# Mask distances built on GpSimd ahead of its first load, and the last store issued from ScalarE's queue for a whole block

## The chip, the core and the metric

One core of a Trainium2 chip. The metric is the device time of one execution in microseconds (us). A single number is the median of several executions. The span that a profile shows is about 2 us shorter than the device time of the same execution (315.6 against 317.4 for the kernel before).

## The reference

Sliding-window attention with ALiBi slopes, then a feed-forward layer with a squared ReLU. Cut to what matters:

```python
# q, k, v: (8 batches, 8 heads, 576 positions, 64), float32
scores = q @ k.T / 8 + slopes * -(i - j)          # only where 0 <= i - j < 128
attn   = softmax(scores) @ v                      # -> x: (4608, 512)
r      = maximum(x @ w_in, 0)                     # w_in: (512, 2048)
out    = (r * r) @ w_out                          # w_out: (2048, 512) -> (4608, 512)
```

576 positions are four blocks of 128 and one of 64 for each batch. The half blocks of two batches share one range of 128 columns of the transposed x.

## The kernel before

The kernel is written as a list of tasks with the engines that may run each, a priority key and dependencies; a small planner orders them ahead of time, and the instructions are emitted in that order. Three places matter here. First, the head: the distances `dist` (key position minus query position) come from an iota on GpSimd. VectorE turns them into the identity for transposes and into the distances with the forbidden side pushed to 1e6; ScalarE exponentiates them into the masks.

```python
def build_iota():
    nc.gpsimd.iota(dist, pattern=[[-128, 2], [1, 128]], base=128, channel_multiplier=-1, ...)
def build_ident():
    nc.vector.tensor_single_scalar(ident, dist[:, 1], 0.0, op=ALU.is_equal)
def build_dist(part):                              # part 1 in the head, part 0 about 18 us later
    op, lim = ((ALU.is_ge, float(window)), (ALU.is_lt, 0.0))[part]
    nc.vector.tensor_scalar(far[:, part], dist[:, part], lim, 1.0e6, op0=op, op1=ALU.mult)
    nc.vector.tensor_tensor(dist[:, part], dist[:, part], far[:, part], op=ALU.add)
```

Second, the loads. Block 0's k and q come through the queues of SyncE and ScalarE into `stage`. Everything else is loaded through GpSimd, which converts float32 to bfloat16 on the way: v of block 0, k, q and v of blocks 1 and 2 ("the seven small loads", 128 KB each as stored), then the weights in quarters of 512 KB (`w_in_sb` is the first of them).

```python
FIRST = ["b0", "b1", "b2", "i0", "i1", "o0", "i2", "o1", "b3", ...]    # b: block, i/o: quarter of w_in/w_out
def fetch_v():
    nc.gpsimd.dma_start(tile_of(s_v[m])[0:n, :, 0:D], source(v, m))
l_v = plan.add({"POOL": 890.0}, key + 0.2, fetch_v, [t_zero] if kb == HALF else [], [s_v[m]], ...)
```

Third, the tail. The last output range is cut into 384 and 128 columns, each evacuated from PSUM and stored by SyncE, with one store for each block in the range. The last range of the kernel before holds the half blocks of the last two batches, so each cut needs two stores of 64 rows.

```python
    jobs.append(("half", [len(seq), len(seq) + 1]))
    ranges.append([(b, HALF), (b + 1, HALF)])
    seq += ranges[-1]
# ... (cut) ...
def store():
    for i, (b, kb) in enumerate(ranges[4 * g + t]):
        n = blk[kb]
        nc.sync.dma_start(out[b * S + kb * 128:b * S + kb * 128 + n, lo:hi], so.tile[i * 64:i * 64 + n, 0:hi - lo])
```

The softmax here doesn't subtract the row's maximum and nothing guards it: scores larger than these inputs give would overflow.

Of the kernel before, what the change touches and what calls it, by code (L numbers as in the profile page):

```python
# [26 lines left out]
CUT = 384  # L27
SIZE = {"kq": 4, "v": 9, "kqT": 7, "P": 3, "x": 3}
DUE = {**{m: 200.0 * m - 1e5 for m in range(40)}, **{7: -40.0}}


def FUSED(g, u):
# [24 lines left out]
class Plan:  # L57
# [24 lines left out]
        return t  # L82

    def order(self):
        used = {tag: [] for tag in self.bufs}
        free, cand, left = {}, {}, {}
        for t in self.tasks:
            left[t] = len(t.deps)
            for d in t.deps:
                d.users.append(t)  # L90
            for e in t.engs:
                free.setdefault(e, self.BEGIN[e])
                cand.setdefault(e, [])
        for t in self.tasks:
            if not left[t]:
                for e in t.engs:
                    cand[e].append(t)

        def avail(t):
            at = t.ready  # L100
            if t.dma is not None:
                lane = self.lanes["SW" if "POOL" in t.engs else "HW"]
                if len(lane) >= self.LANES:
                    at = max(at, lane[-self.LANES])
            taken = {}
            for s in t.acq:
                u, n = used[s.tag], self.bufs[s.tag]
                j = len(u) + taken.get(s.tag, 0) - n
                taken[s.tag] = taken.get(s.tag, 0) + 1
                if j >= len(u):  # L110
                    raise RuntimeError("a task takes more than its ring")
                if j >= 0:
                    if u[j].left:
                        return None
                    at = max(at, u[j].freed)
            return at

        done = []
        n_all = len(self.tasks)
        while len(done) < n_all:  # L120
            best = None
            for e, c in cand.items():
                could = []
                for t in c:
                    a = avail(t)
                    if a is not None:
                        could.append((max(a, free[e]), t.key, t.seq, t))
                lo = None
                if could:
                    by = min(could)[0] + self.NEAR.get(e, 0.0)  # L130
                    got = min((x for x in could if x[0] <= by), key=lambda x: x[1:3])
                    lo = (got[:3], got[3])
                if lo is not None and (best is None or lo[0][:2] < best[0][:2]):
                    best = (lo[0], e, lo[1])
            if best is None:
                raise RuntimeError("plan is stuck: " + repr([
                    (e, t.name, t.key, [s.tag for s in t.acq]) for e, c in cand.items() for t in c][:40]))
            (st, _, _), e, t = best
            t.eng, t.start = e, st
            dur = t.engs[e]  # L140
            if e == "PE" and st < self.FILL_UNTIL:
                t.gap = max(0.0, st - max([free[e]] + [used[s.tag][len(used[s.tag]) - self.bufs[s.tag]].freed
                                                       for s in t.acq if len(used[s.tag]) >= self.bufs[s.tag]]))
            if t.dma is not None:
                at = max(st + self.FIRST[e], self.dma_free)
                self.dma_free = at + t.dma
                t.end = self.dma_free + (self.LAND[e] if t.lat is None else t.lat)
                for _ in range(t.count):
                    self.lanes["SW" if e == "POOL" else "HW"].append(t.end)
            else:  # L150
                t.end = st + dur + (self.LAT[e] if t.lat is None else t.lat)
            free[e] = st + dur
            for x in t.engs:
                cand[x].remove(t)
            for s in t.acq:
                s.idx = len(used[s.tag]) % self.bufs[s.tag]
                used[s.tag].append(s)
            for s in t.rel:
                s.left -= 1
                s.freed = max(s.freed, t.end)  # L160
            for u in t.users:
                left[u] -= 1
                at = st + dur if u.engs.keys() == {e} and t.dma is None else t.end
                if "SP" in u.engs and t.dma is None:
                    at += self.TO_SP
                u.ready = max(u.ready, at)
                if not left[u]:
                    for x in u.engs:
                        cand[x].append(u)
            done.append(t)  # L170
        done.sort(key=lambda t: (t.start, t.seq))
        return done
# [3 lines left out]
def kernel(  # L176
    ctx: ExitStack, tc: tile.TileContext, q, k, v, moe_w_in, moe_w_out, out
):
    nc = tc.nc
# [20 lines left out]
    for b in range(0, B, 2):  # L200
        for x in [(b + i, kb) for i in range(2) for kb in range(1, HALF)]:
            jobs.append(("full", [len(seq)]))
            seq.append(x)
            ranges.append([x])
        jobs.append(("half", [len(seq), len(seq) + 1]))
        ranges.append([(b, HALF), (b + 1, HALF)])
        seq += ranges[-1]
    at = {x: m for m, x in enumerate(seq)}
    NBLK = len(seq)
    col = {}  # L210
# [86 lines left out]

    def build_dist(part):
        op, lim = ((ALU.is_ge, float(window)), (ALU.is_lt, 0.0))[part]
        nc.vector.tensor_scalar(far[:, part], dist[:, part], lim, 1.0e6, op0=op, op1=ALU.mult)  # L300
        nc.vector.tensor_tensor(dist[:, part], dist[:, part], far[:, part], op=ALU.add)

    t_dist, t_mask, last_mask = [None, None], [[], []], None
    for part in (1, 0):
        key = EARLY + 2 if part else -1e5 + 1100
        t_dist[part] = plan.add({"DVE": 430.0}, key, lambda part=part: build_dist(part), [t_ident], name="dist",
                                later=0.0 if part else 18000.0)
        for p in range(H):
            def build_mask(p=p, part=part):
                nc.scalar.activation(masks[:, p, part], dist[:, part], AF.Exp, bias=0.0,  # L310
                                     scale=-(2.0 ** (-8.0 * (head_at[p] + 1) / H)))
            t_mask[part].append(plan.add({"ACT": act(128)}, key + 1 + p, build_mask, [t_dist[part]], name="mask"))

    def ones(ts):
        for t in ts:
            nc.vector.memset(t[:, :, D:D + 1], 1.0)
    t_ones = [plan.add({"DVE": 320.0}, EARLY + 3, lambda: ones(tiles["v0"][0:2]), name="ones"),
              plan.add({"DVE": 900.0}, -1e5 + 300, lambda: ones(tiles["v0"][2:]), name="ones", later=11000.0),
              plan.add({"DVE": 1200.0}, -1e5 + 900, lambda: ones(tiles["v"]), name="ones", later=20000.0)]


    halves = [m for m in range(NBLK) if seq[m][1] == HALF]
# [34 lines left out]
    def load_block(m, key):  # L357
# [32 lines left out]

        def fetch_v():
            nc.gpsimd.dma_start(tile_of(s_v[m])[0:n, :, 0:D], source(v, m))  # L392
        l_v = plan.add({"POOL": 890.0}, key + 0.2, fetch_v, [t_zero] if kb == HALF else [], [s_v[m]],
                       dma=ns, name=f"lv{m}")
        t_v[m] = [l_v, t_ones[0 if m < 2 else 1 if m < B else 2]]

# [25 lines left out]
    def transpose_kq(m, due):  # L422
# [12 lines left out]
        for i in range(2):  # L435
# [14 lines left out]
            for c0, c1 in pieces:  # L450
                def evac(i=i, st=st, c0=c0, c1=c1, e=len(evs[i])):
# [4 lines left out]
                    else:  # L456
# [1 line left out]
                    copy(evs[i][e], o, src)  # L458
                w = (c1 - c0) * n
                evs[i].append(plan.add({"ACT": act(w), "DVE": dve_p(w, 1 if split else 2)}, due - 58, evac,  # L460
                                       [t_tp[i]] + evs[i], [], [st], name=f"ev{m}.{i}"))
        last["tp"] = t_tp[1]
        t_kqT[m] = [[evs[0][0], evs[1][0]], evs[0] + evs[1]]

# [188 lines left out]
    def relu_square(g, slot, last_mm, key, out_of, fused):  # L653
# [12 lines left out]
        else:  # L666
            srt = Slot("rt")

            def relu():
                srt.tile = work.tile([128, 512], BF16, tag="rt", bufs=3, name="rt")  # L670
                nc.scalar.activation(srt.tile, slot.tile, AF.Relu, bias=0.0, scale=1.0)  # L671
            tr = plan.add({"ACT": act(512)}, key, relu, [last_mm], [srt], [slot], name=f"relu{g}")
            ts = plan.add({"DVE": dve(512, 2)}, key, lambda: square(srt.tile), [tr] + g_sq[g][:1], [], [srt],
                          name=f"sq{g}")
        g_sq[g].append(ts)
        return ts

# [54 lines left out]
    def o_piece(g, t, some, key, z, lo, hi, end):  # L732
# [4 lines left out]
        def emit():  # L737
# [3 lines left out]
            for fc in range(4 * some[0], 4 * some[-1] + 4):  # L741
# [2 lines left out]
        tm = plan.add({"PE": 4 * len(some) * mm(hi - lo)}, key, emit,  # L744
                      [prev] + [x for p in some for x in [t_wout[p]] + sq_of[g, t, p]],
                      [slot] if some[0] == 0 else [], [g_slots[g]] if t == 3 and some[-1] == 3 and end else [],
                      name=f"o{g}.{t}.{some[-1]}")
        o_slots[g, t, z][1] = tm
        if some[-1] < 3:
            return  # L750
# [2 lines left out]
        def evac():  # L753
            so.tile = work.tile([128, d_model], FP32, tag="osb", bufs=3, name="osb")
            copy(te, so.tile[:, 0:hi - lo], slot.tile[:, 0:hi - lo])
        te = plan.add({"ACT": act(hi - lo), "DVE": dve_p(hi - lo)}, key, evac, [tm], [so], [slot], name=f"oe{g}.{t}")

        def store():
            for i, (b, kb) in enumerate(ranges[4 * g + t]):
                n = blk[kb]  # L760
                nc.sync.dma_start(out[b * S + kb * 128:b * S + kb * 128 + n, lo:hi],
                                  so.tile[i * 64:i * 64 + n, 0:hi - lo])
        plan.add({"SP": 530.0}, key, store, [te], [], [so], dma=680.0 * (hi - lo) / 512, lat=1000.0, name=f"st{g}.{t}")

    for i, item in enumerate(work_list):
        {"unit": unit, "fc": fc_step, "o": o_part}[item[0]](*item[1:], 4 * i)
# [36 lines left out]
```

## Time and profile before

| quantity | value |
|---|---|
| device time, median of 6 runs | 317.51 us (317.29 to 317.97) |
| span of the profiled run | 315.6 us |
| PE busy | 306.2 us, 97% |
| first load issued by GpSimd | 1.34 us |
| first weight matmul | 14.34 us |
| last matmul ends | 311.0 us |
| last store lands | 314.5 us |

The page of the kernel before shows the bound. In the first line, busy time and share; in the rows below, the busy share of each fortieth of the span in tenths.

```profile
PE 306.2 (97%) x2810; PEld 176.3 (56%) x2810; DVE 173.4 (55%) x494; ACT 173.5 (55%) x340; POOL 105.4 (33%) x131
...
PE   6989999999999999999999999999999999999994
...
DMA  9999999999999999999999949962211000011112
```

TensorE is at nine tenths or more from the fourth slice to the last but one. What can still be won or lost in a change like this lies in the first three slices and the last one. The first slices are also those in which the DMA engines are busy without a break, so TensorE's head hangs on loads.

The timeline of GpSimd in the kernel before (start, duration, engine, instruction). A load's duration here is the time for which GpSimd issues it, not the transfer:

```profile
0.84 0.34 POOL L287 IOTA dist<- 128x256 f32 x1 [0.39 <-POOLq L787]
1.34 1.03 POOL L392 DMA_DIRECT2D vf<-in_v_dram  x1 [0.16 <-issue]
2.36 0.89 POOL L387 DMA_DIRECT2D kq<-in_k_dram  x1
3.24 0.90 POOL L387 DMA_DIRECT2D kq<-in_q_dram  x1
4.11 0.90 POOL L392 DMA_DIRECT2D vf<-in_v_dram  x1
...
7.57 1.55 POOL L340 DMA_DIRECT2D w_in_sb<-in_moe_w_in_dram  x2
```

From its first load on GpSimd is never idle here: after the first, one load follows another every 0.87 us. The first weight load is the eighth, issued at 7.57 and landed at 14.23. (A load has landed when its data is complete; the "lag" below is the time from the start of its issue to its landing.)

The chain of waits that ended last, in its first 45 us (start, duration, what), goes over these loads:

```profile
0.84 0.34 POOL dist L287
1.18 0.16 issue
1.34 1.03 POOL vf L392
2.37 1.76 POOL kq L387 x2
4.13 0.87 POOL vf L392
5.01 1.75 POOL kq L387 x2
6.76 0.88 POOL vf L392
7.63 0.68 POOL w_in_sb L340
8.31 9.45 DMA w_in_sb<-in_moe_w_in_dram
17.75 0.28 issue
18.04 14.42 DMA w_out_sb<-in_moe_w_out_dram
```

The tail of the kernel before, all engines but TensorE's weight loads, cut to the last output:

```profile
309.48 1.54 PE L742 MATMUL o<-w_out_sb,g 128*128 128x384 bf16 x19
...
310.17 0.56 DVE L271 COPY osb<-o 128x384 f32<-128x384 f32 x1 [1.85 <-PE o L742]
310.75 2.41 SPq L761 DMA_DIRECT2D out_dram<-osb  x4
311.06 0.29 DVE L271 COPY osb<-o 128x128 f32<-128x128 f32 x1 [0.34 <-PE o L742]
```

SyncE issues four stores one after the other, from 310.75 to 313.16. The data of the last one was ready at 311.35, but it was issued only at 312.57. That is 1.55 us after the last matmul.

### The profile page before, as it was taken

The numbers are of one execution on the slowest core, as the hardware profiler recorded it, in microseconds if no ns is written. First come the engines' busy times: TensorE is split into PE (matmuls) and PEld (weight loads), VectorE is DVE, ScalarE is ACT, GpSimd is POOL, SyncE is SP. The second block draws the span as 40 slices with busy tenths as digits, with TensorE's granted clock in tenths as the row PEclk, the third lists the DMA queues.
The fourth block names the chain that finished last, engine by engine and source line by source line (L and its number), as shares of the span: only waits on it lengthen the run. The fifth ranks groups of instructions, "written<-read, shape, count | busy, mean of one in ns | idle before, by whom it ended". The sixth has DMA issues, their size and how long they took to land.

```text
span 315.6 us, 7140 instructions
## 1 busy us (share of the span) xinstructions
PE 306.2 (97%) x2810; PEld 176.3 (56%) x2810; DVE 173.4 (55%) x494; ACT 173.5 (55%) x340; POOL 105.4 (33%) x131
## 2 busy tenths in 40 slices
PE   6989999999999999999999999999999999999994
PEld 2878767667777655555555455545444444444442
DVE  3755567666767667676676666666663222222111
ACT  4676466668566635675655665557743444444300
POOL 8825498643623837206756007200000000000000
PEclk9799999999999999999999999999999999999999
DMA  9999999999999999999999949962211000011112
GB/s 129 190 204 190 169 194 178 141 174 127 208 178 127 172 136 194 160 118 143 160 199 160 145 96 137 190 114 70 50 52 50 35 34 33 35 33 44 57 69 66
DMA packets 164130, 39.14 MB, mean 124 GB/s; under 512 B 154752, under 2 KB 159616, under 8 KB 164096
## 3 DMA queue, kind: packets, MB, share of 16 engines
q0 software_dynamic: 114656, 18.10, 84.3%
q1 hardware_dynamic: 49152, 20.33, 34.3%
q8 instruction: 22, 0.36, 0.5%
q10 hardware_dynamic: 288, 0.26, 0.3%
q14 instruction: 12, 0.10, 0.1%
HBM read 36.70 MB, written 9.44 MB: 146 GB/s over the span
## 4 chain that ended last, share of the span: by engine, by line
PE 86%; DMA 9%; POOL 2%; issue 0%; DVE 0%; POOLq 0%
PE o L742 38%; PE h L716 27%; PE h L700 10%; PE pv L566 6%; PE s L499 5%; DMA w_out_sb<-in_moe_w_out_dram 5%; DMA w_in_sb<-in_moe_w_in_dram 3%; DMA kq<-in_q_dram 2%; POOL kq L387 1%; POOL vf L392 1%; PE tp L443 0%; PE xp L608 0%; POOL w_in_sb L340 0%; POOL dist L287 0%; DVE osb L271 0%
## 5 line engine op out<-in xcount | busy, mean ns | idle before, releaser
L742 PE MATMUL o<-w_out_sb,g 128*128 128x512 bf16 (+2 forms) x592 | 143.0, 373 | 0.3 <-DMA w_out_sb<-in_moe_w_out_dram 0.3
L671 ACT ACTIVATE rt<-h 128x512 bf16<-128x512 f32 x144 | 85.8, 609 | 94.2 <-PE h L716 69.9
L662 DVE TENSOR_TENSOR g<-rt 128x512 bf16<-128x512 bf16 x144 | 60.2, 421 | 75.7 <-ACT rt L671 75.6
L716 PE MATMUL h<-xT,w_in_sb 128*128 128x512 bf16 x384 | 96.7, 379 | 0.0
L742 PEld LDWEIGHTS <-g 128*128 128x128 bf16 x592 | 54.0, 98 | 55.9 <-issue 0.4
L523 ACT ACTIVATE P<-s 128x512 bf16<-128x512 f32 (+1 forms) x136 | 67.0, 582 | 9.0 <-PE s L499 8.9
L716 PEld LDWEIGHTS <-w_in_sb 128*128 128x128 bf16 x384 | 35.2, 98 | 39.3
L531 DVE TENSOR_TENSOR P<-P,masks 128x512 bf16<-128x512 bf16 (+1 forms) x112 | 44.6, 405 | 15.1 <-ACT P L523 10.3
L700 PE MATMUL h<-xT,w_in_sb 128*128 128x128 bf16 (+1 forms) x512 | 46.8, 246 | 1.1 <-ACT rt L671 0.7
L387 POOL DMA_DIRECT2D kq<-in_k_dram x39 | 33.5, 858 | 33.5 <-DMA kqT<-kq 28.2
L392 POOL DMA_DIRECT2D vt<-in_v_dram x32 | 27.0, 847 | 45.8 <-PE pv L566 43.5
L700 PEld LDWEIGHTS <-w_in_sb 128*128 128x128 bf16 x512 | 38.6, 98 | 5.2 <-DMA w_in_sb<-in_moe_w_in_dram 1.4
L387 POOL DMA_DIRECT2D kq<-in_q_dram x39 | 33.5, 859 | 9.1 <-PE h L700 4.8
L588 DVE TENSOR_TENSOR x<-pv,rec 128x256 bf16<-128x256 f32 (+1 forms) x80 | 33.5, 422 | 2.6
L566 PEld LDWEIGHTS <-P 128*128 128x128 bf16 (+1 forms) x576 | 26.0, 101 | 15.2 <-DVE x L588 1.7
L584 DVE RECIPROCAL rec<-pv 128x4 f32<-128x4 f32 (+1 forms) x80 | 14.2, 179 | 21.0 <-PE pv L566 18.1
L566 PE MATMUL pv<-vt,P 128*128 128x65 bf16 (+1 forms) x448 | 24.6, 194 | 0.0
L273 ACT ACTIVATE osb<-o 128x512 f32<-128x512 f32 x23 | 13.9, 606 | 8.0 <-PE o L742 7.7
L499 PEld LDWEIGHTS <-kqT 64*128 64x128 bf16 x448 | 12.4, 94 | 7.3 <-issue 7.2
L271 DVE COPY osb<-o 128x512 f32<-128x512 f32 (+2 forms) x14 | 9.2, 654 | 12.8 <-PE o L742 12.6
L499 PE MATMUL s<-kqT 64*128 64x128 bf16 (+1 forms) x256 | 15.6, 210 | 0.0
L499 PE MATMUL s<-kqT,kqT 64*128 64x128 bf16 (+1 forms) x192 | 11.4, 209 | 0.0
(42 smaller groups left out, 103.1 us busy)
## 6 DMA issues: line engine op xcount, KB each, us to landing
out_dram<-osb SPq DMA_DIRECT2D x32, 256.0 KB, 4.0
kq<-in_k_dram POOLq DMA_DIRECT2D x31, 128.0 KB, 7.2
kq<-in_q_dram POOLq DMA_DIRECT2D x31, 128.0 KB, 7.4
vt<-in_v_dram POOLq DMA_DIRECT2D x24, 128.0 KB, 7.4
w_in_sb<-in_moe_w_in_dram POOLq DMA_DIRECT2D x4, 512.0 KB, 11.0
w_out_sb<-in_moe_w_out_dram POOLq DMA_DIRECT2D x4, 512.0 KB, 14.4
vf<-in_v_dram POOLq DMA_DIRECT2D x8, 128.0 KB, 6.7
out_dram<-osb SPq DMA_DIRECT2D x6, 128.0 KB, 2.3
```

The lines of the kernel that those rows point to most:

```text
L387: nc.gpsimd.dma_start(view(kq[s_kq[m].idx], i), source(src, m, split))
L392: nc.gpsimd.dma_start(tile_of(s_v[m])[0:n, :, 0:D], source(v, m))
L499: nc.tensor.matmul(sS[2 * g2 + r].tile[:, jj * 256 + c0:jj * 256 + c0 + w], tile_of(s_kqT[mk])[rows, c, :], tile_of(s_kqT[mq])[rows, C + c ...
L523: nc.scalar.activation(flat(Pt[sP.idx]), sS[i].tile.rearrange("p (j t) -> p j t", j=2)[:, :, lo:hi], AF.Exp, bias=0.0, scale=scale)
L531: nc.vector.tensor_tensor(flat(Pt[sP.idx]), flat(Pt[sP.idx]), flat(masks), op=ALU.mult)
L566: nc.tensor.matmul(sv.tile[0:n, hi * (D + 1):(hi + 1) * (D + 1)], Pt[sP.idx][:, place(h)].rearrange("p t q -> p (t q)")[:, w], tile_of(s_v ...
L588: nc.vector.tensor_tensor(xt[sx.idx][0:n, hf * 256:(hf + 1) * 256].rearrange("p (h e) -> p h e", h=4), heads(sv)[0:n, :, 0:D], sr.tile[0:n ...
L662: nc.vector.tensor_tensor(o, i, i, op=ALU.mult)
L671: nc.scalar.activation(srt.tile, slot.tile, AF.Relu, bias=0.0, scale=1.0)
L700: nc.tensor.matmul(slot.tile[:, f * w:(f + 1) * w], w_in_sb[:, cc, fc * 128:(fc + 1) * 128], xT[:, cc, lo:lo + w], start=cc == 0, stop=cc ...
L716: nc.tensor.matmul(slot.tile, w_in_sb[:, cc, fc * 128:(fc + 1) * 128], xT[:, cc, g * 512:(g + 1) * 512], start=cc == 0, stop=cc == C - 1)
L742: nc.tensor.matmul(slot.tile[:, 0:hi - lo], gt[:, fc, t * 128:(t + 1) * 128], w_out_sb[:, fc, lo:hi], start=fc == 0, stop=fc == FCB - 1)
```

## The change

The intent: in the tail, let the last range be a whole block (one store for each cut instead of two) and let ScalarE, which is idle by then, evacuate the last 128 columns and store them from its own queue. In the head, take the two instructions for the distances off VectorE and put them on GpSimd between its iota and its first load. The core of the diff, cut and with long lines shortened; the rest renames tasks, removes an unused variable and adds an empty table of priority offsets:

```diff
         jobs.append(("half", [len(seq), len(seq) + 1]))
-        ranges.append([(b, HALF), (b + 1, HALF)])
-        seq += ranges[-1]
+        seq += [(b, HALF), (b + 1, HALF)]
+        ranges.insert(len(ranges) - (b + 2 == B), seq[-2:])
 ...
     def build_dist(part):
         op, lim = ((ALU.is_ge, float(window)), (ALU.is_lt, 0.0))[part]
-        nc.vector.tensor_scalar(far[:, part], dist[:, part], lim, 1.0e6, op0=op, op1=ALU.mult)
-        nc.vector.tensor_tensor(dist[:, part], dist[:, part], far[:, part], op=ALU.add)
+        e = nc.gpsimd if part else nc.vector
+        e.tensor_scalar(far[:, part], dist[:, part], lim, 1.0e6, op0=op, op1=ALU.mult)
+        e.tensor_tensor(dist[:, part], dist[:, part], far[:, part], op=ALU.add)
 ...
-        t_dist[part] = plan.add({"DVE": 430.0}, key, lambda part=part: build_dist(part), [t_ident], name="dist",
-                                later=0.0 if part else 18000.0)
+        t_dist[part] = plan.add({"POOL": 700.0} if part else {"DVE": 430.0}, key, lambda part=part: build_dist(part),
+                                [t_iota if part else t_ident], name=f"dist{part}", later=0.0 if part else 18000.0)
 ...
-        l_v = plan.add({"POOL": 890.0}, key + 0.2, fetch_v, [t_zero] if kb == HALF else [], [s_v[m]],
+        l_v = plan.add({"POOL": 890.0}, key + 0.2, fetch_v, [t_zero] if kb == HALF else [t_dist[1]], [s_v[m]],
 ...
-        te = plan.add({"ACT": act(hi - lo), "DVE": dve_p(hi - lo)}, key, evac, [tm], [so], [slot], ...)
+        engs = {"ACT": act(hi - lo), "DVE": dve_p(hi - lo)}
+        if end and (g, t) == (NG - 1, 3):
+            del engs["DVE"]
+        te = plan.add(engs, key, evac, [tm], [so], [slot], ...)
+        final = end and (g, t) == (NG - 1, 3)
 ...
-                nc.sync.dma_start(out[...], so.tile[...])
-        plan.add({"SP": 530.0}, key, store, ...)
+                (nc.scalar if final else nc.sync).dma_start(out[...], so.tile[...])
+        plan.add({"ACTQ" if final else "SP": 530.0}, key, store, ...)
```

A comparison of the built programs shows that the order of TensorE's instructions is the same in both kernels. The two distance instructions are the only ones that move in the head, and the last copy and the last stores the only ones in the tail.

More of the change, by code (lines that the diff above doesn't have):

```diff
@@ L29 @@
 DUE = {**{m: 200.0 * m - 1e5 for m in range(40)}, **{7: -40.0}}
+ADJ = {}
 def FUSED(g, u):
@@ L84, in order @@
     def order(self):
+        for t in self.tasks:
+            t.key += ADJ.get(t.name, 0.0)
         used = {tag: [] for tag in self.bufs}
@@ L299, in build_dist @@
         op, lim = ((ALU.is_ge, float(window)), (ALU.is_lt, 0.0))[part]
-        nc.vector.tensor_scalar(far[:, part], dist[:, part], lim, 1.0e6, op0=op, op1=ALU.mult)
-        nc.vector.tensor_tensor(dist[:, part], dist[:, part], far[:, part], op=ALU.add)
-    t_dist, t_mask, last_mask = [None, None], [[], []], None
+        e = nc.gpsimd if part else nc.vector
+        e.tensor_scalar(far[:, part], dist[:, part], lim, 1.0e6, op0=op, op1=ALU.mult)
+        e.tensor_tensor(dist[:, part], dist[:, part], far[:, part], op=ALU.add)
+    t_dist, t_mask = [None, None], [[], []]
     for part in (1, 0):
         key = EARLY + 2 if part else -1e5 + 1100
-        t_dist[part] = plan.add({"DVE": 430.0}, key, lambda part=part: build_dist(part), [t_ident], name="dist",
-                                later=0.0 if part else 18000.0)
+        t_dist[part] = plan.add({"POOL": 700.0} if part else {"DVE": 430.0}, key, lambda part=part: build_dist(part),
+                                [t_iota if part else t_ident], name=f"dist{part}", later=0.0 if part else 18000.0)
         for p in range(H):
@@ L311, in build_mask @@
                                      scale=-(2.0 ** (-8.0 * (head_at[p] + 1) / H)))
-            t_mask[part].append(plan.add({"ACT": act(128)}, key + 1 + p, build_mask, [t_dist[part]], name="mask"))
+            t_mask[part].append(plan.add({"ACT": act(128)}, key + 1 + p, build_mask, [t_dist[part]], name=f"mask{part}.{p}"))
     def ones(ts):
@@ L316, in ones @@
             nc.vector.memset(t[:, :, D:D + 1], 1.0)
-    t_ones = [plan.add({"DVE": 320.0}, EARLY + 3, lambda: ones(tiles["v0"][0:2]), name="ones"),
-              plan.add({"DVE": 900.0}, -1e5 + 300, lambda: ones(tiles["v0"][2:]), name="ones", later=11000.0),
-              plan.add({"DVE": 1200.0}, -1e5 + 900, lambda: ones(tiles["v"]), name="ones", later=20000.0)]
+    t_ones = [plan.add({"DVE": 320.0}, EARLY + 3, lambda: ones(tiles["v0"][0:2]), name="ones0"),
+              plan.add({"DVE": 900.0}, -1e5 + 300, lambda: ones(tiles["v0"][2:]), name="ones1", later=11000.0),
+              plan.add({"DVE": 1200.0}, -1e5 + 900, lambda: ones(tiles["v"]), name="ones2", later=20000.0)]
     halves = [m for m in range(NBLK) if seq[m][1] == HALF]
@@ L460, in transpose_kq @@
                 evs[i].append(plan.add({"ACT": act(w), "DVE": dve_p(w, 1 if split else 2)}, due - 58, evac,
-                                       [t_tp[i]] + evs[i], [], [st], name=f"ev{m}.{i}"))
+                                       [t_tp[i]] + evs[i], [], [st], name=f"ev{m}.{i}.{c0}"))
         last["tp"] = t_tp[1]
@@ L671, in relu @@
                 nc.scalar.activation(srt.tile, slot.tile, AF.Relu, bias=0.0, scale=1.0)
-            tr = plan.add({"ACT": act(512)}, key, relu, [last_mm], [srt], [slot], name=f"relu{g}")
+            tr = plan.add({"ACT": act(512)}, key, relu, [last_mm], [srt], [slot], name=f"relu{last_mm.name}")
             ts = plan.add({"DVE": dve(512, 2)}, key, lambda: square(srt.tile), [tr] + g_sq[g][:1], [], [srt],
-                          name=f"sq{g}")
+                          name=f"sq{last_mm.name}")
         g_sq[g].append(ts)
@@ L746, in o_piece @@
                       [slot] if some[0] == 0 else [], [g_slots[g]] if t == 3 and some[-1] == 3 and end else [],
-                      name=f"o{g}.{t}.{some[-1]}")
+                      name=f"o{g}.{t}.{some[-1]}" + ("b" if z else ""))
         o_slots[g, t, z][1] = tm
@@ L755, in evac @@
             copy(te, so.tile[:, 0:hi - lo], slot.tile[:, 0:hi - lo])
-        te = plan.add({"ACT": act(hi - lo), "DVE": dve_p(hi - lo)}, key, evac, [tm], [so], [slot], name=f"oe{g}.{t}")
+        engs = {"ACT": act(hi - lo), "DVE": dve_p(hi - lo)}
+        if end and (g, t) == (NG - 1, 3):
+            del engs["DVE"]
+        te = plan.add(engs, key, evac, [tm], [so], [slot], name=f"oe{g}.{t}.{z}")
+        final = end and (g, t) == (NG - 1, 3)
         def store():
@@ L760, in store @@
                 n = blk[kb]
-                nc.sync.dma_start(out[b * S + kb * 128:b * S + kb * 128 + n, lo:hi],
-                                  so.tile[i * 64:i * 64 + n, 0:hi - lo])
-        plan.add({"SP": 530.0}, key, store, [te], [], [so], dma=680.0 * (hi - lo) / 512, lat=1000.0, name=f"st{g}.{t}")
+                (nc.scalar if final else nc.sync).dma_start(
+                    out[b * S + kb * 128:b * S + kb * 128 + n, lo:hi], so.tile[i * 64:i * 64 + n, 0:hi - lo])
+        plan.add({"ACTQ" if final else "SP": 530.0}, key, store, [te], [], [so], dma=680.0 * (hi - lo) / 512,
+                 lat=1000.0, name=f"st{g}.{t}.{z}")
     for i, item in enumerate(work_list):
```

## The prediction

> **What bounds it now.** TensorE: the page's busy table gives PE 306.2 us of a 315.6 us span (97%), granted clock 0.995. The rest is the head (PE waits until about 37 us) and the tail after the last matmul. The chain that ended last shows the head: iota on GpSimd (0.84 to 1.18 us), seven GpSimd-issued loads back to back (0.87 to 1.03 each), a weight load landing at 17.75, another issued at 18.04 landing at 32.46, one more landing near 42.6; then PE runs unbroken to 311.04. The slices show DMA at 9 tenths from the third slice to 43 us.
>
> **What moves.** PE's instruction order is unchanged; the other engines' lists differ only at the two ends.
>
> *Tail.* Before (timeline and the output tile's view): last matmul ends 311.04; VectorE copies 128x128 in 0.29, to 311.35. SyncE's queue is then behind: the last range was two half blocks, so the 384 columns went as two stores (issues 310.75, 311.3) and the 128 columns as two (312.0, 312.6); issues of 64 rows take 0.49 to 0.59, against 0.33 for 128 rows. The last, issued at 312.57, landed 1.9 later, 314.5; 1.1 us of closing follows. After: one 384-column store on SyncE at 310.75; ScalarE copies the last 128 columns (estimate 0.27, from its 0.60 for 512 and 0.38 for 256) and issues one store from its idle queue at about 311.4. Landing 2.0 later: 313.4, so 1.1 us less, all critical. The trace's 1.9 to 2.1 to landing agrees with the Trainium skill, "DMA: Bandwidth & Descriptors", anatomy of one DMA, which calls about 2.0 us fixed: only the queueing can be saved.
>
> *Head.* Two 128x128 fp32 instructions leave VectorE (0.22 and 0.29, in slack: it next waits for a load until 3.75) and enter GpSimd between iota and the first load. The trace has none like them on GpSimd; the skill's "GPSIMD Engine Reference", elementwise cycle accounting, gives 1.03 cycles per element for one input, about 2.6 for two, at 1.2 GHz: 0.11 + 0.28, plus two dispatches and semaphore waits, estimate 0.7 us (0.5 to 0.9). All GpSimd-issued loads start that much later. Masks end about 5.1 to 5.3 either way and are needed at 8.65: nothing gained. The delay is partly absorbed: the software queue flows thinly until 5 us, while the first k and q (hardware queues, 0.52 MB) still move, then is at its limit, one 128 KB load landing each 0.85 to 0.9 us. With later competition the q pieces, landing at 6.2, should land 0.3 to 0.7 earlier. I estimate the weight loads 0.45 us later (0.1 to 0.75); PE waits for them at 14.3, 17.8, 22.3 and 32.5, so all of PE shifts by about that.
>
> **Sum.** -1.1 + 0.45 = about -0.65 us, 0.2%. Predicted 316.9 us, 8 in 10 between 316.2 and 317.5. Faster by over 2%: 0.005; within 2%: 0.99; slower: 0.005.
>
> **What would show it.** GpSimd's first load starting near 2.0 instead of 1.34; the first weight matmul near 14.7 instead of 14.31, the second w_in wait ending near 18.2; PE's last matmul near 311.5; the last store issued within 0.4 us of it, on ScalarE's queue; last landing near 2.4 us after the last matmul instead of 3.4.
>
> **What would make it wrong.** GpSimd's elementwise work costing over 1 us, or its port being held up by VectorE's ident; the whole 0.7 us, or none, passing through the DMA stage (it may even help if q gains); ScalarE's store being slow to issue or land (its first issue took 0.64); a closing longer than 1.1 us.

## The result, and the profile after

The changed kernel takes 318.11 us (317.58 to 318.69, 6 runs) against 317.51 us (317.29 to 317.97, 6 runs). Ratios here and below are the mean time of one kernel's fast runs over that of the other's in the same rounds, so they are not quite the ratio of the medians. The ratio is 1.0017, with a 95% interval of 1.0002 to 1.0032: slightly slower, where 0.65 us less was predicted, and outside the predicted range.

The page after, the same rows:

```profile
PE 301.8 (96%) x2768; PEld 175.1 (55%) x2810; DVE 172.2 (55%) x491; ACT 173.8 (55%) x341; POOL 106.8 (34%) x133
...
PE   6599999999999999999999999999999999999996
...
DMA  9999999999999999998999929981121100010022
```

PE's second slice (about 8 to 16 us) fell from 9 to 5 tenths and its last slice rose from 4 to 6: a loss in the head and a gain in the tail. (The smaller count of PE's instructions is records missing from the trace; the weight-load count is unchanged.)

GpSimd's timeline in the changed kernel:

```profile
0.84 0.34 POOL L292 IOTA dist<- 128x256 f32 x1 [0.40 <-POOLq L799]
1.28 0.64 POOL L306 TENSOR_SCALAR far<-dist 128x128 f32<-128x128 f32 x1
2.00 0.45 POOL L307 TENSOR_TENSOR dist<-dist,far 128x128 f32<-128x128 f32 x1
2.40 1.10 POOL L398 DMA_DIRECT2D vf<-in_v_dram  x1
3.50 1.07 POOL L393 DMA_DIRECT2D kq<-in_k_dram  x1
4.56 0.88 POOL L393 DMA_DIRECT2D kq<-in_q_dram  x1
...
8.89 1.55 POOL L346 DMA_DIRECT2D w_in_sb<-in_moe_w_in_dram  x2
```

The first load starts at 2.40 instead of 1.34, which is 1.06 us later. The first two loads also take longer to issue (1.10 and 1.07 us instead of 1.03 and 0.89), so that the first weight load is issued 1.32 us later. The chain of waits takes the same way as before, later at each step:

```profile
8.94 0.69 POOL w_in_sb L346
9.63 9.57 DMA w_in_sb<-in_moe_w_in_dram
19.20 0.28 issue
19.48 14.97 DMA w_out_sb<-in_moe_w_out_dram
```

TensorE's timeline around the first weight matmul, in the kernel before and in the changed kernel; the bracket is the idle time before the instruction and what ended it:

```profile
14.34 1.05 PE L700 MATMUL h<-xT,w_in_sb 128*128 128x128 bf16 x16
```

```profile
13.50 0.28 PE L572 MATMUL pv<-vf,P 128*128 128x65 bf16 x4
16.13 1.07 PE L706 MATMUL h<-xT,w_in_sb 128*128 128x128 bf16 x16 [2.35 <-DMA w_in_sb<-in_moe_w_in_dram]
```

The attention of block 0 was done earlier than before, and TensorE stood idle for 2.35 us for the first weights, which landed at 16.09 instead of 14.23. From there on everything is shifted: the last matmul ends at 312.80 instead of 311.02, 1.78 us later.

The tail of the changed kernel:

```profile
311.94 0.56 DVE L276 COPY osb<-o 128x384 f32<-128x384 f32 x1 [1.85 <-PE o L748]
312.84 0.28 ACT L278 ACTIVATE osb<-o 128x128 f32<-128x128 f32 x1 [13.26 <-PE o L748]
313.14 0.35 ACTq L772 DMA_DIRECT2D out_dram<-osb  x1
```

The last store is issued 0.34 us after the last matmul and lands at 314.71. From the last matmul to the end of the span it takes 3.12 us, before it was 4.61. So the two profiles add up: 1.78 lost in the head, 1.49 won in the tail, 0.29 more in the span (315.92 against 315.63).

### The profile page after: what moved, and what is told of

It reads as the page before. It is cut to its first block, busy times and chain, and to the rows that moved or that the text cites. A ratio compares the mean times of both kernels' runs of the same rounds, so it can differ in the third digit from the quotient of the medians.

```text
span 315.9 us, 7097 instructions
## 1 busy us (share of the span) xinstructions
PE 301.8 (96%) x2768; PEld 175.1 (55%) x2810; DVE 172.2 (55%) x491; ACT 173.8 (55%) x341; POOL 106.8 (34%) x133
## 4 chain that ended last, share of the span: by engine, by line
PE 87%; DMA 8%; POOL 3%; issue 1%; ACT 0%; POOLq 0%
PE o L748 38%; PE h L722 26%; PE h L706 10%; PE pv L572 6%; PE s L505 5%; DMA w_out_sb<-in_moe_w_out_dram 5%; DMA w_in_sb<-in_moe_w_in_dram 3%; POOL kq L393 1%; POOL vf L398 1%; PE tp L449 1%; PE xp L614 0%; POOL w_in_sb L346 0%; POOL far L306 0%; POOL dist L307 0%; POOL dist L292 0%
## 5 line engine op out<-in xcount | busy, mean ns | idle before, releaser
L748 PE MATMUL o<-w_out_sb,g 128*128 128x512 bf16 (+2 forms) x567 | 138.5, 373 | 2.9 <-issue 1.6
L722 PE MATMUL h<-xT,w_in_sb 128*128 128x512 bf16 x367 | 95.5, 379 | 0.8
L393 POOL DMA_DIRECT2D kq<-in_k_dram x39 | 33.7, 865 | 31.7 <-DMA kqT<-kq 24.9
L278 ACT ACTIVATE osb<-o 128x512 f32<-128x512 f32 (+1 forms) x24 | 14.2, 593 | 21.2 <-PE o L748 20.9
L276 DVE COPY osb<-o 128x512 f32<-128x512 f32 (+1 forms) x13 | 8.9, 681 | 12.5 <-PE o L748 12.3
```

The source lines that it names most:

```text
L393: nc.gpsimd.dma_start(view(kq[s_kq[m].idx], i), source(src, m, split))
L722: nc.tensor.matmul(slot.tile, w_in_sb[:, cc, fc * 128:(fc + 1) * 128], xT[:, cc, g * 512:(g + 1) * 512], start=cc == 0, stop=cc == C - 1)
L748: nc.tensor.matmul(slot.tile[:, 0:hi - lo], gt[:, fc, t * 128:(t + 1) * 128], w_out_sb[:, fc, lo:hi], start=fc == 0, stop=fc == FCB - 1)
```

## The experiments

Each kernel was timed in five rounds against the kernel before on the same chip, profiled once, and gave the correct result. The edits shown are cut: declarations of scratch tiles and the planner's bookkeeping are left out. They are against the kernel before, and in all of them the order of TensorE's instructions is that of the kernel before.

### First four: which part does what

Theory A says that the change is two independent parts that add, a gain in the tail and a loss in the head. **Tail alone:** the range, evacuation and store edits of the diff, nothing in the head.

> Tail edits alone (whole last block, ScalarE evacuates and stores the last 128 columns), GpSimd head as before. Theory A (the change is two independent parts, tail gain and head loss, that add): PE's last matmul stays at 311.0 +- 0.3 us, the time from it to the end falls from 4.59 us to the 3.08 us seen in the changed kernel, so ratio about 0.9953 (1.5 us less, about 316.0). Rival B (the changed kernel's later PE end comes from the tail edits too, for instance the swapped column ranges): PE ends later than 311.5 here as well and the ratio is 0.998 or more.

Measured: 316.19 us, ratio 0.9956 (0.9944 to 0.9969). PE ends at 310.64, a touch below the 311.0 +- 0.3 expected, and the end follows 3.13 us later. Otherwise as theory A expected; rival B falls.

**Head alone:** the `build_dist` and `fetch_v` edits, nothing in the tail.

> GpSimd builds the mask distances ahead of its first load, tail as before. Theory A: first GpSimd load starts near 2.4 instead of 1.34, first weight matmul near 16.1 instead of 14.31, PE ends 1.8 us or more later (312.8 or more), ratio 1.006 to 1.008 (about 2 to 2.5 us more). Rival B: the head costs only its 1.06 us of later start, ratio about 1.003.

Measured: 319.53 us, ratio 1.0061 (1.0049 to 1.0074); first load at 2.41, first weight matmul at 16.09, PE ends at 312.78. The two ratios multiplied give 0.9956 x 1.0061 = 1.0017, the ratio of the whole change.

**Whole last block alone:**

```diff
-        ranges.append([(b, HALF), (b + 1, HALF)])
-        seq += ranges[-1]
+        seq += [(b, HALF), (b + 1, HALF)]
+        ranges.insert(len(ranges) - (b + 2 == B), seq[-2:])
```

> Only the range order is changed, so that the last 128 rows are one block; both pieces still evacuated by VectorE and stored from SyncE's queue. Theory A1 (the saving is the number of stores in SyncE's queue): the queue is free again at about 311.1, before the last copy ends at 311.35, so the last store goes out at once and the whole 1.5 us is had without ScalarE: ratio 0.995 to 0.996. Rival (a second queue is needed): ratio 0.998 or more.

Measured: 316.19 us, ratio 0.9959 (0.9946 to 0.9973). Its tail:

```profile
310.59 0.56 DVE L271 COPY osb<-o 128x384 f32<-128x384 f32 x1 [1.85 <-PE o L742]
311.17 0.97 SPq L761 DMA_DIRECT2D out_dram<-osb  x2
311.48 0.29 DVE L271 COPY osb<-o 128x128 f32<-128x128 f32 x1 [0.34 <-PE o L742]
```

Two stores instead of four, and SyncE's queue is free when the last copy ends: the store is issued 0.36 us after the last matmul, from ScalarE in the kernel with the whole tail 0.35. From the last matmul to the end it takes 3.13 us in both. ScalarE's queue adds nothing once the last range is a whole block.

**ScalarE's queue alone**, with two half blocks in the last range:

```diff
+        engs = {"ACT": act(hi - lo), "DVE": dve_p(hi - lo)}
+        if end and (g, t) == (NG - 1, 3): del engs["DVE"]
-                nc.sync.dma_start(out[...], so.tile[...])
+                (nc.scalar if final else nc.sync).dma_start(out[...], so.tile[...])
```

> Only the last piece's evacuation and store move to ScalarE; the last range is still two half blocks, so ScalarE issues two 64-row stores, at about 311.4 and 312.0. Theory A1: about half of the saving, 0.6 us, ratio 0.998. Rival (queue matters, count does not): 1.5 us, ratio 0.995.

Measured: 317.06 us, ratio 0.9987 (0.9975 to 1.0000). ScalarE issues two 64-row stores, 0.35 and 0.93 us after the last matmul, and the last lands 3.09 after it (3.46 in the kernel before, 1.91 with one store). 4.24 us from the last matmul to the end: 0.36 us won in the profile, less than the 0.6 expected, because these two stores also took longer to land (2.16 us for the last, against 1.91 in the kernel before).

### Next four: how 1.06 us of GpSimd time became 1.8 us

**The same two instructions, for nothing.** VectorE builds the distances as before; GpSimd runs the pair on scratch tiles ahead of its first load.

```diff
         def fetch_v():
+            if m == 0:
+                nc.gpsimd.tensor_scalar(scr[:, 0], dist[:, 0], 0.0, 1.0e6, op0=ALU.is_lt, op1=ALU.mult)
+                nc.gpsimd.tensor_tensor(scr[:, 1], dist[:, 0], scr[:, 0], op=ALU.add)
             nc.gpsimd.dma_start(tile_of(s_v[m])[0:n, :, 0:D], source(v, m))
```

> VectorE builds the distances as before; GpSimd runs the same two instructions on scratch tiles that nobody reads, ahead of its first load (tail as before). Theory A (the loss is GpSimd's time ahead of its loads and nothing else): the same loss as with the real move, ratio 1.005 to 1.0075, first weight matmul 15.8 to 16.4 us. Rival C (the loss comes from what waits for GpSimd's result: identity, masks, VectorE's order): ratio under 1.002.

Measured: 319.92 us, ratio 1.0069 (1.0046 to 1.0092), first weight matmul at 16.25. The same loss as with the real move: nothing that waits for the distances matters. Rival C falls.

**The pair twice.** The two added lines are there two times.

> The scratch pair twice, about 2.1 us of GpSimd time ahead of the first load. Theory A1 (without a backlog in the software queue, descriptor generation sets the pace, so further delay passes on one to one): 1.0 to 1.2 us more than the single pair, ratio 1.009 to 1.011. Rival D (the first 1.06 us was amplified to 1.75 by something that repeats, such as the load lanes): 1.75 us more, ratio 1.012 or above.

Measured: 320.61 us, ratio 1.0086 (1.0065 to 1.0107), first load at 3.70, first weight matmul at 17.14, PE ends at 313.39. The second 1.26 us of delay cost about 0.5 us by the ratios and by PE's end. Both expectations are missed by the measured ratio. Rival D (amplification that repeats, 1.012 or above) lies outside the interval and falls; theory A1 (one to one, 1.009 to 1.011) lies partly inside it and is not excluded. The intervals of the single and the double pair overlap, so that the second microsecond costs less than the first is likely but not shown.

**The pair behind the third load.** The real distances on GpSimd, but after k and q of block 1 have been issued:

```diff
         def fetch_kq():
             for i, src in enumerate((k, q)):
                 nc.gpsimd.dma_start(view(kq[s_kq[m].idx], i), source(src, m, split))
+            if m == 1:
+                build_dist(1)
```

> GpSimd builds the distances, but after its third load instead of ahead of its first (tail as before); it is the same GpSimd time ahead of the weight loads. Theory A1 in its plain form (generation sets the pace everywhere, position does not matter): weight load issued near 8.9, ratio 1.005 to 1.007 as with the pair in front. Theory A2 (the 5 us between issue and landing in the kernel before hold a backlog of finished descriptors that the engines drain at 1227 packets per us; a pause behind it is hidden, in front of it is not): ratio 1.000 to 1.003, first weight matmul before 15.2.

Measured: 319.66 us, ratio 1.0065 (1.0048 to 1.0082), first weight matmul at 16.99. Theory A2, which I held more likely, falls in the form given: the backlog that exists at that time does not hide the pause (1.23 us without a load being issued, from 4.17 to 5.40). A1's ratio is met. The profile, which is of the slowest of the six executions (320.57 us), shows the engines slower after the pause. The transfers between 6 and 10 us of the kernel before, then of this one (packets started, bytes, rate; a packet is the piece of a transfer that the trace records, 128 bytes for the small loads):

```profile
DMA packets 4891, 0.62 MB, mean 154 GB/s; under 512 B 4891, under 2 KB 4891, under 8 KB 4891
```

```profile
DMA packets 3838, 0.48 MB, mean 121 GB/s; under 512 B 3838, under 2 KB 3838, under 8 KB 3838
```

Issuing goes on at one load per 0.87 us after the pause, but within this stretch the engines do not get back to their former rate: 1175, 975, 800 and 888 packets start in its four microseconds, against 1212 to 1227 in the kernel before. Between 10 and 11 us it is 1193 again.

**The other direction.** With the whole last block, and the iota moved behind GpSimd's first load, to get the first load out earlier:

```diff
-    t_iota = plan.add({"POOL": 400.0}, EARLY + IOTA, build_iota, name="iota")
+    t_iota = plan.add({"POOL": 400.0}, EARLY + IOTA, lambda: None, name="iota")
...
             nc.gpsimd.dma_start(tile_of(s_v[m])[0:n, :, 0:D], source(v, m))
+            if m == 0:
+                build_iota()
```

> The other direction: the iota, too, goes behind GpSimd's first load, which then starts near 0.84 instead of 1.34; tail as in the run with the whole last block alone (316.19 us). Theory A1: 0.5 us less, ratio 0.9940 to 0.9950. Theory A2 (in the kernel before the engines already drain a backlog at their limit from 5 us on): little is gained, 0 to 0.25 us, ratio 0.9952 to 0.996.

Measured: 317.16 us, ratio 0.9980 (0.9963 to 0.9997), so about 0.7 us worse than the same tail without it (0.9959, 0.9946 to 0.9973; the intervals overlap a little). Both theories missed. The first load could not start at 0.84; it started at 1.25. The iota then took 0.4 us between the first and the second load, the first weight load was issued 0.26 us later than with the same tail and the old head (8.08 against 7.82), and the first weight matmul came 1.12 us later (15.31 against 14.19). In this profile a pause of a few tenths loses more than it lasts.

### Last three: late start, dose and place

Theory A3, made from these, and still a theory: what counts is whether GpSimd stays far enough ahead of the DMA engines; when it does not, the engines fall below their rate and the weights behind the small loads come late by more than the pause.

**Waiting instead of working.** GpSimd does no elementwise work; its first load waits for VectorE, which runs four short memsets first.

```diff
+            if m == 0:
+                for _ in range(3):
+                    nc.vector.memset(scr, 0.0)
+                nc.vector.memset(tile_of(s_v[m])[0:n, :, 0:D], 0.0)
             nc.gpsimd.dma_start(tile_of(s_v[m])[0:n, :, 0:D], source(v, m))
```

> No elementwise work on GpSimd; its first load waits instead on VectorE, which runs four short memsets first (the last one on the tile that the load fills), so the load starts near 2.4 us as in the changed kernel, with GpSimd idle. Theory A3 (what counts is how late the first load starts, because the software queue then never builds the backlog that lets the engines run at 1227 packets per us): first weight matmul 15.7 to 16.4, ratio 1.005 to 1.007. Rival E (elementwise work on GpSimd itself slows the descriptor work after it): ratio 1.003 or less.

Measured: 319.83 us, ratio 1.0063 (1.0046 to 1.0079). The first load started at 2.84, later than planned, and the first weight matmul at 16.89, after the range expected. GpSimd that idles costs about as much as GpSimd that works, so rival E falls in the form given (1.003 or less). That the work has no cost of its own is not shown: the idle start came 1.50 us late for this ratio, the busy ones 1.07 to 1.10.

**Half the dose.** Only the two-operand instruction ahead of the first load, on scratch tiles.

> Only one scratch instruction (the two-operand one, 0.45 us, with its wait about 0.55 us) ahead of GpSimd's first load. Theory A3: the loss is not proportional to the delay but steps up when the backlog is lost; with the first load near 1.9 the small loads lag their issue by 4.3 to 4.6 us and the loss is over half of the full one, ratio 1.003 to 1.006. Rival F (proportional, 1.75 us per 1.06 us): 0.9 us, ratio 1.0028, with lags between.

Measured: 318.39 us, ratio 1.0029 (1.0005 to 1.0053), six runs from 317.11 to 320.27. The first load started at 1.65, not 1.9: the one instruction moved it by only 0.31 us. The interval holds both expectations, so this run decides nothing between a step and a proportion. What it shows is scatter: 3.2 us between executions of one program, where the kernel before scatters by 0.85 us in the same rounds. (In the rounds of the second set of runs the kernel before itself scattered by 1.66 us, 317.14 to 318.80.)

**The same work where the queue is deep.** The scratch pair behind GpSimd's second weight load.

```diff
                 nc.gpsimd.dma_start(w_in_sb[:, :, n * w:(n + 1) * w], ...)
+                if n == 1:
+                    nc.gpsimd.tensor_scalar(scr[:, 0], dist[:, 0], 0.0, 1.0e6, op0=ALU.is_lt, op1=ALU.mult)
+                    nc.gpsimd.tensor_tensor(scr[:, 1], dist[:, 0], scr[:, 0], op=ALU.add)
```

> The scratch pair after GpSimd's second weight load, where the queue holds more than 9 us of work, instead of ahead of the first load. Theory A3: hidden, ratio 0.999 to 1.0015, first weight matmul 14.0 to 14.5. Rival E or the plain form A1 (GpSimd time in the head costs wherever it stands): ratio 1.003 or more.

Measured: 317.52 us, ratio 0.9996 (0.9984 to 1.0008), PE ends at 311.08. First weight matmul at 14.55, a touch after the range. No loss is seen, as theory A3 expected: the weight quarter just ahead of the pair lands 8.3 us after its issue, so the engines have work enough. That the first weights are issued before the pair, and so cannot be late, is not the whole of it: the quarter of w_out right behind the pair was issued 1.31 us later than in the kernel before (10.35 against 9.04) and landed at 19.70 against 19.74. Its transfers between 6 and 10 us are those of the kernel before:

```profile
DMA packets 4901, 0.62 MB, mean 154 GB/s; under 512 B 4901, under 2 KB 4901, under 8 KB 4901
```

### All heads side by side

Times in us, each from the one profile of that kernel. "Packets" are those started between 6 and 10 us. "Last step" is from the landing of the seventh small load to that of the first weight quarter, both from the landing records in the trace. Such a record holds 16 time stamps for each load, without the name of an engine, and the last of them is the landing; "first stamp" and "spread" are the first of them for the first weight quarter and the time from it to the last. The profiles of "waiting" and of "pair behind the third load" are of the slowest executions of their kernels, 0.6 and 0.9 us above the medians.

| kernel | first load issued | packets | first weights issued, landed | last step | first stamp, spread | PE ends |
|---|---|---|---|---|---|---|
| before | 1.34 | 4891 | 7.57, 14.23 | 2.53 | 13.20, 1.03 | 311.02 |
| tail alone | 1.34 | 4891 | 7.58, 13.97 | 2.53 | 12.97, 1.00 | 310.64 |
| whole block alone | 1.34 | 4889 | 7.82, 14.14 | 2.53 | 13.04, 1.10 | 311.44 |
| ScalarE's queue alone | 1.35 | 4902 | 7.77, 13.99 | 2.53 | 12.91, 1.08 | 311.22 |
| pair where the queue is deep | 1.35 | 4901 | 7.59, 14.10 | 2.54 | 12.96, 1.14 | 311.08 |
| half the dose | 1.65 | 4599 | 8.15, 15.59 | 2.60 | 13.40, 2.19 | 311.69 |
| iota behind the first load | 1.25 | 4672 | 8.08, 15.26 | 3.44 | 13.45, 1.81 | 312.11 |
| the change | 2.40 | 4343 | 8.89, 16.09 | 3.08 | 14.23, 1.85 | 312.80 |
| head alone | 2.41 | 4174 | 8.91, 16.04 | 3.50 | 14.29, 1.75 | 312.78 |
| scratch pair | 2.44 | 4270 | 8.97, 16.20 | 3.87 | 14.40, 1.80 | 312.89 |
| waiting | 2.84 | 4092 | 9.06, 16.84 | 4.06 | 14.58, 2.27 | 314.01 |
| pair behind the third load | 1.35 | 3838 | 8.96, 16.95 | 4.15 | 14.33, 2.61 | 314.20 |
| pair twice | 3.70 | 3778 | 10.27, 17.09 | 3.06 | 15.70, 1.40 | 313.39 |

The kernels fall into two groups. Where GpSimd issues its first seven loads from 1.34 on without a pause, about 4890 to 4900 packets start in those 4 us and the first weight quarter needs 2.53 us after the last small load. Everywhere else there are fewer packets (in the last row partly because the loads start so late) and the weights need up to 4.2 us; with half the dose the time is lost one load earlier, between the sixth and the seventh (2.00 us). PE's end follows the landing of the first weights, within some 0.6 us.

The stamps split the loss. In the changed kernel the first stamp of the first weights comes 1.03 us later than before, which is the late start of the first load (1.06) passed on whole, and the spread grows from 1.03 to 1.85 us. So does it elsewhere: wherever the first load itself started later than in the kernel before, the first stamp is later by about as much, to within 0.2 us, and in all eight kernels with a pause ahead of the weights the spread is 1.40 to 2.61, against 1.00 to 1.14 in the other five. With half the dose, 15 of the 16 stamps are in by 14.38 and the last one comes at 15.59. What the loss has beyond the delay itself is thus that the parts of one load finish further apart.

## Why the prediction was wrong

**The tail's mechanism was right, its size was not.** The saving was predicted as 1.1 us and measured as 1.49 in the profiles; the tail alone measures a ratio of 0.9956, about 1.4 us. The issue of the last store came 1.21 us earlier after the last matmul (1.55 to 0.34), as costed. The term that was off is the landing: I took "Landing 2.0 later" from stores of the kernel before, which landed 1.85 to 2.19 us after their issue, while the 64 KB store of 128 rows landed 1.57 us after its issue. Also, the credit went to ScalarE's idle queue; the whole-block run shows that the count of stores in SyncE's queue is all of it.

**The head is where it failed**: it was costed at 0.45 us and PE's end moved by 1.78. Two terms were wrong; that the work could cost over 1 us, and that the whole delay could pass, the prediction had named as risks, a loss beyond the delay it had not. The first is "estimate 0.7 us (0.5 to 0.9)" for the GpSimd work. It was 1.06 us: the instruction with a scalar operand took 0.64 us and the two-operand one 0.45, with waits between. The Trainium skill, "GPSIMD Engine Reference", section on elementwise cycle accounting, gives 1.03 cycles per element for one input, from which my estimate was 0.11 us for 128 elements at 1.2 GHz, with only dispatch and waits put on top. The trace does not agree at this size: this was about a sixth of the 0.64 us that the scalar one took. For the two-operand one the estimate was 0.28 us plus dispatch, against 0.45.

The second term is the larger: "The delay is partly absorbed ... I estimate the weight loads 0.45 us later". The first small load does bear out the absorption: issued 1.06 us later, it landed at 6.32, even before the 6.65 of the kernel before, because block 0's q on the hardware queue was done by 5.11 instead of 6.15. But then the step fails. In the kernel before, the small loads land 0.78 to 0.95 us apart, and lag their issue by 5.0 to 5.3 us. In the changed kernel the distances from the second landing on are 0.84, 0.83, 0.99, 1.10 and 1.37 us, and the weights follow 3.08 us after the last. I had read from the profile that the queue "is at its limit", and took this limit as given in the changed kernel too. The reading that the runs fit is that the limit was reached only because GpSimd had stayed ahead of the engines, and that the change took that lead away. The lead was small. Loads that found little ahead of them (the first of "waiting" and of "pair twice", the fourth of "pair behind the third load") still landed 3.49 to 3.55 us after their issue, so of the lag of 5.0 to 5.3 us I estimate about 1.5 us as lead, and the pauses took 1.06 to 1.26 of it. Between 6 and 10 us the rate fell from 4891 to 4343 packets, 154 to 137 GB/s; in the changed kernel:

```profile
DMA packets 4343, 0.55 MB, mean 137 GB/s; under 512 B 4343, under 2 KB 4343, under 8 KB 4343
```

So the delay was not absorbed but grew, from 1.06 us at the first load to 1.86 at the landing of the first weights, and PE's end moved by 1.78.

**What was right:** that VectorE's release and the masks gain nothing, that q gains (it landed 1.04 us earlier, more than the 0.3 to 0.7 said), that TensorE waits for the weights and passes the shift on to its end, and that the change is within 2%. The signs named for the head all pointed to the error: first load at 2.40 (said: near 2.0), first weight matmul at 16.13 (near 14.7), last matmul at 312.80 (near 311.5). Those for the tail came true or better: the last store issued 0.34 us after the last matmul (said: within 0.4), and landed 1.91 after it (near 2.4).

**What stays open.** That a delay of the small loads is not absorbed is shown by the head alone, by the scratch pair, by the late start with idle GpSimd and by the pause behind the third load, and in all but the late start the measured ratio is clearly more than the delay itself; that a pause can be free is shown where the queue is deep. That the lost lead is the reason is argued from these, and the run meant to tell a step from a proportion (half the dose) decided nothing. Why fewer packets start and the stamps of one load spread is not shown. The packets themselves are not slower: their times between 6 and 10 us add up to 242.0% of 16 engines' time for 4891 packets before and 215.0% for 4343 after (over 100% because packets overlap), which gives 31.7 ns for a packet in both. So fewer packets are under way at a time. The lag from issue to landing, above 4 us for most small loads in the changed kernel, does not settle whether loads were lacking, since a load with little ahead of it takes 3.5 us as well. The Trainium skill, "DMA: Bandwidth & Descriptors", section on latency and other measured facts, guesses that two of the 16 engines are slowed by the traffic of the descriptor rings that GpSimd fills. Uneven engines would fit the wider spread of the stamps, but the traces here do not name the engines, and in the changed kernel it is not two stamps alone that are late: the eighth of the sixteen of the first weights moved by 1.47 us (13.51 to 14.98), the first by 1.03. Also open is the scatter of the kernels with a late head: six runs of the scratch pair spread over 2.6 us; why one execution loses more than another was not followed. (Six runs of the changed kernel spread over 1.1 us, no more than the kernel before did in some rounds.)

**A better kernel.** The tail without the head beats both kernels: 316.19 us. The three lines for the whole last block alone give as much (316.19 us, ratio 0.9959), and are the version to keep.

## What to carry to other kernels

Where an engine feeds a queue of many small loads that the critical work waits for, do not count on the queue to absorb a pause ahead of them. Look at how far the engine is ahead: the time from issue to landing, less the time that a load needs with nothing in front of it. Here a lag of 4.7 us, of which some 3.5 were that time, did not hide a pause of 1.23 us; a lag of 8.3 us hid one of about the same length. "The engines are at their limit" is then a state that the present order of issues produces, not a property that a changed order can count on. At the end of a kernel, count the stores queued behind the last matmul before looking for a second queue.

## What the Trainium skill lacked or had wrong

- "GPSIMD Engine Reference", section on engine selection, calls one-input elementwise work on GpSimd roughly line-rate. Here a 128x128 fp32 instruction with two scalar operations took 0.64 us on GpSimd and 0.22 us on VectorE, and more than the two-operand add on GpSimd (0.45 us). The page has no duration for such short instructions with a scalar operand, and no run here tells a rate from a fixed time per instruction.
- "DMA: Bandwidth & Descriptors" gives a bandwidth by size for loads issued from GpSimd, but not that a train of them slows when GpSimd starts it late or pauses in it: 4889 to 4902 packets of the small loads in 4 us without that, 3778 to 4672 with it, and 512 KB landing 2.53 us after the load before it against up to 4.15.
- The same page's fixed cost of about 2.0 us is fitted to DMAs issued from GpSimd; it has no such fit for stores from SyncE and ScalarE. Here a 64 KB store to HBM from the queue of SyncE or ScalarE landed 1.54 to 1.57 us after its issue, a 256 KB one 1.97.
- No page that I found says that a store of 64 rows takes longer to issue than one of 128: 0.49 to 0.59 us on SyncE and 0.56 and 0.84 on ScalarE, against 0.33 to 0.35 on both.
